# A planned attention and gated feed-forward kernel: new landing estimates for the first transfers and a new table of urgencies

## The chip, the cores and the metric

The kernel runs on one core of one Trainium2 chip. The metric is the device time of one execution in microseconds, as the median of several timed runs. A separate execution, with the hardware profiler on, gives the profile and the trace.

## What is computed

Two parts follow one another. The first is attention without a softmax: queries and keys are projected by two small matrices, the outer product of the two projections is the feature vector of 64 numbers, and the output is a quotient of two sums over keys. The second is a gated feed-forward layer whose gate mixes the rows of the sequence.

```python
def phi(x):
    a = einsum('rd,bhsd->bhsr', S1, x); b = einsum('rd,bhsd->bhsr', S2, x)
    return einsum('bhsi,bhsj->bhsij', a, b).reshape(..., r * r)
kv = einsum('bhsf,bhsd->bhfd', phi(k), v); z = phi(k).sum(2)
x  = (phi(q) @ kv) / (phi(q) @ z + 1e-6)        # heads side by side: (4, 1088, 128)

h = maximum(x @ w_in, 0);  u, v = h[..., :512], h[..., 512:]
v_n = (v - mean(v)) / sqrt(var(v) + 1e-6)
v_s = einsum('ts,bsd->btd', w_spatial, v_n) + b_spatial[:, None]
out = (u * v_s) @ w_out
```

There are 4 batches, 4 heads, 1088 rows, head width 32, model width 128 and hidden width 1024.

## The kernel before

**The work.** Matrices that need full precision are split into a high half (a cast to fp32r) and a low half (the difference). A product is then three matmuls: high by high, high by low, low by high (`mm3`, L439 to L441). Most of the time goes to the spatial product: for each batch b, each block d of 128 gate columns and each group c of output columns (424, 332 and 332 wide), nine k tiles of W are run through, with lines L1011 (high by high), L1013 (low half of v), L1020 and L1022 (low half of W). The tiles of W, their high halves (ScalarE, L563) and low halves (L566, VectorE or GpSimd) are made once, at the beginning. The weights w_in, w_out and the projection matrices arrive as 64-bit numbers, and VectorE makes 32-bit ones of them in some seven instructions (L501 to L514, the first of them on ScalarE for large ones); then come the high half (L518, ScalarE) and the low half (L449, VectorE).

**Batch 0** is prepared with nothing to hide it. Its attention goes through projections (L591), features (L596 on ScalarE, L598 on VectorE), sums over keys (L629), transposes (L717, copied out by L721), sums over features (L731), a division (L735 to L738), a second transpose (L745) and the split of x into halves (L749 on ScalarE, L750 on VectorE). This is done in three groups of 384 rows. Each group then gives three hidden tiles of v (`hidden_v`: `mm3` of 512 columns into the banks `sd`, the ReLU L865 on ScalarE, statistics L867 and L868, the normalization L871 to L890). For batch 0 the normalized tile becomes vh (L955, ScalarE) and vl (L958, VectorE or GpSimd), one k tile after another, and the spatial product of the first column group runs over all four blocks, d = 0 to 3, at once. The gate halves u are products into the one bank `pu`, which ScalarE empties (L1003). Early projections of the queries of batch 1 (L764) stand in the same stretch. L466 is dummy work that keeps PE running where the plan sees it wait.

**Later batches.** Their attention is done beside the spatial product of the batch before. Projected queries go out to memory and come back spread over partitions (the tiles `abd`; L772, L780, L783), GpSimd multiplies them (L784) and makes the low half (L452), and PE uses them in `mm3` into `sd`.

**What sets the order.** Nobody writes the order by hand. Each piece of work is an operation with an engine, a cost, its inputs and outputs and, for PE's main work, a due time. `Order.schedule` first carries the due times backwards to all operations, and takes from each one's due time the value of the table `LEADS` for its name and its group (`o.lead`). It then runs a list scheduler with its own model of the engines: of the operations that can start, each engine takes the one with the earliest due time. Loads (`load`, L446, on the queue of SP) are modelled by their size, one after the other, with eight in flight. The result is one fixed order of instructions for each engine, and a fixed buffer for each tile; the hardware only waits on semaphores. A number in the model or in `LEADS` so changes the order of instructions and nothing else. The assignment of an operation to one of two engines is made by the same planner.

Of the kernel before, what the change touches and what calls it, by code (L numbers as in the profile page):

```python
# [11 lines left out]
U32 = mybir.dt.uint32  # L12
# [65 lines left out]
class T:  # L78
# [8 lines left out]
    @property  # L87
    def ap(self):
        if self._ap is None:
            self._ap = self.k.place(self)  # L90
        return self._ap
# [32 lines left out]
class Order:  # L124
# [13 lines left out]
    def op(self, eng, cost, fn, r=(), w=(), due=None, kb=0, alts=(), sh=False, kind=None, after=0.0, lead=0.0, f4=False, cls=None, lag=0.0):  # L138
# [8 lines left out]
        if kind:  # L147
            o.alts = tuple(a for a in o.alts if a[0] in FORCE.get(kind, [eng]))
            o.eng, _, o.fn = o.alts[0]
            assert o.alts, kind  # L150
        o.stretch, o.sh, o.after, o.lead = self.stretch, sh, after * 1e3, lead + sum(LEADS.get(x, 0) for x in (*self.part, o.name))
        deps = {}
# [49 lines left out]
    def schedule(self):  # L202
# [25 lines left out]
        dma, slow = 0.0, False  # L228
# [5 lines left out]
        while left:  # L234
            best = None
            for e, os in avail.items():
                can = []
                lo = 1e18
                for o in os:
                    s = max(free[e], self.ready_at(o, e))  # L240

                    if e == "POOL":
                        s = max(s, shared_to - 40)
# [5 lines left out]
                    for tag, ts in need.items():  # L249
                        n = len(ts)  # L250
# [3 lines left out]
                        s = max(s, slots[tag][n - 1][0])  # L254
# [3 lines left out]
                if can:  # L258
                    d, s, n, o = min((o.due + STICK * (e == "PE" and o.cls != cls), s, o.n, o) for s, o in can if s <= lo + SLACK[e])
# [4 lines left out]
            s, e, o = best  # L264
            if len(o.alts) > 1:
                s, e = min((self.could_end(o, a, free), a[0]) for a in o.alts)
                s = max(free[e], self.ready_at(o, e), best[0] if e == best[1] else 0)
            _, cost, fn = next(a for a in o.alts if a[0] == e)
            if e == "PE" and s < FILL_TO * 1e3:

                n = int((s - free[e] - FILL_SPARE) // (FILL if s > COLD_TO else FILL_COLD))
# [10 lines left out]
            if e == "PE":  # L282

                s += TURN * (o.f4 != f4)
                f4 = o.f4
                if o.cls != cls or s > free[e] + PAUSE:
                    run = 0
                cls, run = o.cls, run + o.nmm
                settle = SETTLE.get(cls, (0,))
                cost += settle[min(run, len(settle) - 1)] - settle[min(run - o.nmm, len(settle) - 1)]  # L290
                o.end = s + cost + 165
                free[e] = s + cost
            elif e == "SP":
                dma = max(dma, s + cost + 1950) + o.kb / (0.38 if o.kb > 0 else -0.12)

                if dma > 5000 and not slow:
                    slow, dma = True, dma + 1900
                o.end = dma + o.lag
                lanes.append(o.end)
                free[e] = max(s + cost, lanes[-8] if len(lanes) >= 8 else 0)  # L300
            else:
                o.end = s + cost

                if e == "DVE" and o.sh and pool_busy[0] <= s < pool_busy[1] - 20:
                    o.end = max(o.end, pool_busy[1] + cost - 60)
                if e == "POOL":
                    pool_busy = (s, o.end)
                if e == "DVE" and o.sh:
                    shared_to = o.end
                free[e] = o.end - self.OV[e]  # L310
# [36 lines left out]
def c_act(n, psum=False, ptr=False):  # L347
    return (157 if psum else 190) + 0.833 * n + (190 if ptr else 0) if n > 16 else 203


def c_dve(n):
    return 152 + 1.045 * n
# [6 lines left out]
def c_pool(n):  # L359
    return 90 + 2.4 * n  # L360
# [7 lines left out]
def tile_kernel(ctx: ExitStack, tc: tile.TileContext, kT, qT, vA, sks, idn, msk, wT, w_in, w_out, bsp, out):  # L368
# [62 lines left out]
    k = Order(place)  # L431
# [3 lines left out]
    def bank(tag, name):  # L435
        return tl(tag, name, [P, 512])
# [6 lines left out]
    def load(t, ap, src, kb, w=None, **kw):  # L443
        if t.name in FIRST:
            kw["due"] = FIRST.index(t.name) - 1e4
        op("SP", 470, lambda: nc.sync.dma_start(out=ap(), in_=src), w=[w or t], kb=kb, **kw)  # L446

    def sub(o, a, bb):
        return lambda: nc.vector.tensor_tensor(out=o(), in0=a(), in1=bb(), op=ALU.subtract)  # L449

    def sub_pool(o, a, bb):
        return lambda: nc.gpsimd.tensor_tensor(out=o(), in0=a(), in1=bb(), op=ALU.subtract)  # L452
# [3 lines left out]
    z9 = tl(None, "z9", [P, P])  # L456
# [3 lines left out]
    wps = bank("sd", "wps")  # L460
# [9 lines left out]
    eps = tl(None, "eps", [P, 2])  # L470
# [9 lines left out]
    NSK = 2 * H * R  # L480
# [34 lines left out]

    def split(hi, lo, x, n, r, wh, wl, pool=False, due=None, alt=False):

        op("ACT", c_act(n), lambda: nc.scalar.copy(out=hi(), in_=x()), r=r, w=wh)  # L518
        if pool:
            op("POOL", c_pool(n), sub_pool(lo, x, lambda: hi().bitcast(F32)), r=[*r, *wh], w=wl, due=due)  # L520
        else:
            alts = [("POOL", c_pool(n), sub_pool(lo, x, lambda: hi().bitcast(F32)))] if alt else []
            op("DVE", c_dve(n), sub(lo, x, lambda: hi().bitcast(F32)), r=[*r, *wh], w=wl, due=due, sh=True, alts=alts)

    sk = tl(None, "sk", [P, 2 * NSK])
    s_raw = tl("pl", "s_raw", [P, 384])
    load(s_raw, lambda: s_raw[:, :2 * NSK].bitcast(U32), sks.bitcast(U32), 64)
    from_f64(sk, s_raw, NSK)
    ident = tl("abT", "ident_sb", [P, P])
    load(ident, lambda: ident.ap, idn, 64)  # L530

    mask = tl(None, "mask_sb", [P, 6])
    load(mask, lambda: mask.ap, msk, 2)

    kd0 = tl("abT", "kd0", [P, 2, 2, D + 1])

    wTh = tl(None, "wTh", [P, NS, S], F32R)
    wTl = tl(None, "wTl", [P, NS, S], F32R)
    wih = [tl(None, f"wih{j}", [P, DH], F32R) for j in range(2)]
    wil = [tl(None, f"wil{j}", [P, DH], F32R) for j in range(2)]  # L540
    woh = tl(None, "woh", [P, ND, DM], F32R)
    wol = tl(None, "wol", [P, ND, DM], F32R)


    def load_wi(j, raw, x):
        sl = slice(j * 512, j * 512 + 512)
        load(raw, lambda: raw[:, :1024].bitcast(U32), w_in[:, sl].bitcast(U32), 524)
        from_f64(x, raw, 512)
        split(lambda: wih[j].ap, lambda: wil[j].ap, lambda: x[:, :512], 512, [(x, "x")], [wih[j]], [wil[j]])
# [554 lines left out]
    k.part = ("wi1",)  # L1104

    load_wi(1, tl("vt", "wi_raw1", [P, 1024]), tl("vt", "wi_x1", [P, 1024]))
    attention0(sts[0])
    st = sts[0]
# [3 lines left out]
    load_bias()  # L1112
    k.part = ("wi0",)
    load_wi(0, Whole(k, "kt", "wi_raw0", [P, 384]), Whole(k, "v", "wi_x0", [P, 396]))
    k.part = ("wo",)
    load_wo(Whole(k, "kt", "wo_raw", [P, 384]), Whole(k, "v", "wo_x", [P, 396]))
# [62 lines left out]
```

## Time and profile before

| | |
|---|---|
| median of the timed runs | 327.97 us (327.59, 327.98, 327.97) |
| the profiled execution | 328.65 us |
| its span, first to last instruction | 326.8 us |
| TensorE's granted clock in it | 0.999 |
| busy: PE, VectorE, ScalarE, GpSimd | 319.2, 194.3, 152.3, 49.6 us |
| bytes moved | 23.97 MB, 73 GB/s on average |

The clock is full throughout. Busy times of PE are modelled from the starts of pipelined matmuls, so they include the time in which a matmul drains while the next one runs, and small waits hide in them. Columns of transfers and engines by time show a first stretch of some 45 us in which loads, the attention of batch 0 and the preparation of W share all engines, and a long stretch behind it in which PE runs the spatial products.

### The profile page before, as it was taken

Reading aid. Unit: us, or ns where it says so; the run is one execution under the profiler, and the core shown is the slowest. Engines: PE = TensorE matmul, PEld = TensorE weight load, DVE = VectorE, ACT = ScalarE, POOL = GpSimd, SP = SyncE. Lnnn points to the kernel's source line nnn. Section 1 sums busy time; section 2 is a strip of 40 time slices with the busy share of each in tenths; the row PEclk is TensorE's granted clock in tenths of the full one; section 3 lists DMA queues with packets and bytes.
Section 4 is the critical chain, followed back from the end, with each engine's and each line's share of the span. In section 5 each row is a group of like instructions: output and inputs, shape, how many; then the busy total and the mean of one; then the engine's idle time right before and its main releaser. Section 6 shows DMA issues by size and latency. Waiting matters only on the chain.

```text
span 326.8 us, 6680 instructions
## 1 busy us (share of the span) xinstructions
PE 319.2 (98%) x2663; PEld 304.8 (93%) x2663; DVE 194.3 (59%) x437; ACT 152.3 (47%) x358; POOL 49.6 (15%) x60
## 2 busy tenths in 40 slices
PE   8989999999999999999999999999999999999996
PEld 7977899989999899899899999899999999999995
DVE  4889998447689962489984083699544141131023
ACT  2389866634766455366543182764243132121122
POOL 1000100778201005530000730200000000000000
PEclk9999999999999999999999999999999999999999
DMA  6952059674011253400123311000000001000001
GB/s 190 301 170 73 18 157 288 207 214 136 0 38 54 80 179 96 127 2 24 47 70 112 118 41 42 0 2 0 2 1 0 2 27 44 0 0 2 0 2 68
DMA packets 18961, 23.97 MB, mean 73 GB/s; under 512 B 2546, under 2 KB 18674, under 8 KB 18930
## 3 DMA queue, kind: packets, MB, share of 16 engines
q1 hardware_dynamic: 18930, 23.54, 23.5%
q8 instruction: 21, 0.34, 0.5%
q14 instruction: 10, 0.08, 0.1%
HBM read 20.46 MB, written 3.06 MB: 72 GB/s over the span
## 4 chain that ended last, share of the span: by engine, by line
PE 72%; DMA 10%; ACT 5%; DVE 4%; POOL 3%; SPq 2%; issue 2%; POOLq 0%; ACTq 0%
PE sp L1011 16%; PE sp L1020 15%; PE sp L1013 15%; DMA pl<-abd 4%; DMA pl<-in_wT 4%; PE sd L440 3%; PE sd L439 2%; PE sd L441 2%; PE po L439 2%; PE po L441 2%; PE po L440 2%; PE pu L439 2%; DMA v<-in_vA 2%; PE sp L1022 2%; PE pu L441 2%
## 5 line engine op out<-in xcount | busy, mean ns | idle before, releaser
L1011 PE MATMUL sp<-wT,vh 128*128 128x332 f32 (+1 forms) x414 | 133.7, 323 | 0.0
L1013 PE MATMUL sp<-wT,vl 128*128 128x332 f32 (+1 forms) x368 | 118.6, 322 | 0.4 <-DVE vl L958 0.4
L1020 PE MATMUL sp<-wT,vh 128*128 128x332 f32 (+1 forms) x368 | 116.9, 322 | 0.0
L1011 PEld LDWEIGHTS sp<-wT,vh 128*128 128x128 f32 x414 | 77.8, 188 | 1.4 <-issue 0.6
L1013 PEld LDWEIGHTS sp<-wT,vl 128*128 128x128 f32 x368 | 69.2, 188 | 1.2 <-DVE vl L958 0.7
L1020 PEld LDWEIGHTS sp<-wT,vh 128*128 128x128 f32 x368 | 69.0, 188 | 0.2
L1047 DVE TENSOR_TENSOR u<-sp,u 128x332 f32<-128x332 f32 (+1 forms) x40 | 20.6, 517 | 56.4 <-PE sp L1022 47.6
L1003 ACT ACTIVATE u<-pu 128x332 f32<-128x332 f32 (+1 forms) x40 | 18.5, 462 | 30.4 <-PE pu L441 27.7
L867 DVE BATCH_NORM_STATS2 st<-vt 128x6 f32<-128x512 f32 x36 | 24.4, 689 | 11.9 <-ACT vt L865 11.6
L518 ACT CAST g<-u 128x332 fp32r<-128x332 f32 (+1 forms) x38 | 18.1, 484 | 28.3 <-DVE u L1047 18.9
L449 DVE TENSOR_TENSOR g<-u,g 128x332 fp32r<-128x332 f32 (+1 forms) x38 | 20.3, 533 | 15.7 <-PE po L440 9.9
L865 ACT ACTIVATE vt<-sd 128x512 f32<-128x512 f32 x36 | 21.2, 598 | 16.7 <-PE sd L441 16.3
L845 DVE RECIPROCAL c<-c 128x384 f32<-128x384 f32 (+1 forms) x9 | 21.8, 2419 | 7.8 <-ACT c L843 7.6
L784 POOL TENSOR_TENSOR pl<-pl,pl 128x384 f32<-128x384 f32 (+1 forms) x18 | 18.1, 1012 | 53.3 <-DMA pl<-abd 53.3
L927 ACT CAST vh<-vt 128x384 fp32r<-128x384 f32 x36 | 17.7, 510 | 13.3 <-DVE vt L887 10.7
L452 POOL TENSOR_TENSOR r<-pl,r 128x384 fp32r<-128x384 f32 (+1 forms) x18 | 18.6, 1039 | 27.5 <-ACT r L518 27.5
L929 DVE TENSOR_TENSOR vl<-vt,vh 128x384 fp32r<-128x384 f32 (+1 forms) x36 | 17.8, 506 | 2.0 <-ACT vh L927 1.5
L518 ACT CAST r<-pl 128x384 fp32r<-128x384 f32 (+1 forms) x18 | 8.8, 493 | 18.7 <-POOL pl L784 15.3
L598 DVE TENSOR_TENSOR kp<-ka,sd 128x768 f32<-128x768 f32 x15 | 13.7, 948 | 6.0 <-DMA out<-kp 3.6
L563 ACT CAST wT<-pl 128x332 fp32r<-128x332 f32 (+1 forms) x27 | 13.1, 497 | 7.9 <-DMA pl<-in_wT 7.6
L439 PE MATMUL pu<-x,wih 128*128 128x332 f32 (+1 forms) x48 | 16.4, 341 | 0.3 <-ACT u L1003 0.2
L887 DVE TENSOR_SCALAR vt<-vt,mv,sm 128x512 f32<-128x512 f32 x32 | 15.8, 539 | 0.0
(154 smaller groups left out, 500.7 us busy)
## 6 DMA issues: line engine op xcount, KB each, us to landing
pl<-in_wT SPq DMA_DIRECT2D x18, 166.0 KB
v<-in_vA SPq DMA_DIRECT2D x12, 198.0 KB
kt<-in_kT SPq DMA_DIRECT2D x12, 192.0 KB
pl<-abd SPq DMA_DIRECT2D x12, 192.0 KB
pl<-abd SPq DMA_DIRECT2D x24, 96.0 KB
pl<-in_wT SPq DMA_DIRECT2D x9, 212.0 KB
c<-in_qT SPq DMA_DIRECT2D x7, 192.0 KB
out<-u SPq DMA_DIRECT2D x6, 166.0 KB
```

What stands on the lines that cost most here:

```text
L439: nc.tensor.matmul(o, ah, bh, start=start, stop=False)
L441: nc.tensor.matmul(o, al, bh, start=False, stop=stop)
L449: return lambda: nc.vector.tensor_tensor(out=o(), in0=a(), in1=bb(), op=ALU.subtract)
L452: return lambda: nc.gpsimd.tensor_tensor(out=o(), in0=a(), in1=bb(), op=ALU.subtract)
L518: op("ACT", c_act(n), lambda: nc.scalar.copy(out=hi(), in_=x()), r=r, w=wh)
L845: op("DVE", 135 + 6.3 * n, lambda x32=x32, n=n: nc.vector.reciprocal(out=x32[:, :n], in_=x32[:, :n]), w=[x32])
L865: op("ACT", c_act(512, True) + 16, lambda pv=pv, t=t: nc.scalar.activation(vt[:, t], pv.ap, AF.Relu), r=[pv], w=[(vt, t)])
L867: op("DVE", 690, lambda stats=stats, t=t: nc.vector.bn_stats(out=stats.ap, in_=vt[:, t]), r=[(vt, t)], w=[stats])
L1011: nc.tensor.matmul(sp[:, :cw], vh[:, kt], wTh[:, kt, cs], start=(kt == 0), stop=False)
L1013: nc.tensor.matmul(sp[:, :cw], vl[:, kt], wTh[:, kt, cs], start=False, stop=False)
L1020: nc.tensor.matmul(sp[:, :cw], vh[:, kt], wTl[:, kt, cs], start=False, stop=False)
L1047: op("DVE", c_dve(cw), lambda: nc.vector.tensor_tensor(out=u.ap, in0=sp[:, :cw], in1=u.ap, op=ALU.mult), r=[sp], w=[u], lead=LEAD[1])
```

## The change

Three numbers of the planner's model of the transfers are other ones, and the table of urgencies is a new one. It had 1577 entries and has 1581; of the 1748 names in the two, 1739 have another value. The table is one line; its first entries stand for it here.

```diff
-LEADS = {'W0': -5650, 'W0.0': 9780, 'W0.1': -16100, 'W0.2': -13770, 'W0.3': 10920,
...
+LEADS = {'W0': -19300, 'W0.0': 11900, 'W0.2': -16500, 'W0.3': 14820, 'W0.4': 2800,
...
                 if dma > 5000 and not slow:
-                    slow, dma = True, dma + 1900
+                    slow, dma = True, dma + 1400
...
-    load(s_raw, lambda: s_raw[:, :2 * NSK].bitcast(U32), sks.bitcast(U32), 64)
+    load(s_raw, lambda: s_raw[:, :2 * NSK].bitcast(U32), sks.bitcast(U32), 64, lag=-800, due=-1e6)
...
-        load(raw, lambda: raw[:, :1024].bitcast(U32), w_in[:, sl].bitcast(U32), 524)
+        load(raw, lambda: raw[:, :1024].bitcast(U32), w_in[:, sl].bitcast(U32), 1000 if j else 1160)
```

The load of the projection matrices is planned to land 0.8 us sooner and to be issued first; the two halves of w_in are planned as if they had 1000 and 1160 KB (they have 512 KB each, as before); a delay that the plan adds once, early, is 1.4 us and was 1.9.

The same instructions run on the same engines, but for three pairs of normalizations of batch 0 (L887 on VectorE, L890 on ScalarE) that change places, and for the dummies L466, 16 and not 17. The order of the first loads is nearly what it was. The order on the engines differs in many places. Three of them follow.

ScalarE, in the attention of batch 0, behind the copies of the first transposes (`ka`, the last feature copy; `wih`, the high half of the second half of w_in; `kt` and `v`, where the first half of w_in lands and is converted; `c`, copies of transposes; `wT`, high halves of W; `x`, the high half of x). Before:

```order
L596 COPY ka_69<-sd_91 128x96
L501 ACTIVATE v<-kt 128x512
L518 CAST wih_280<-vt_165 128x512
L563 CAST wT<-pl_213 128x424
L518 CAST bh<-b_64 83x16
L563 CAST wT<-pl_229 128x424
L563 CAST wT<-pl_238 128x424
L721 COPY c_112<-po_266 128x384
L721 COPY c_146<-po_148 128x384
L563 CAST wT<-pl_251 128x424
L749 CAST x<-sp_308 128x384
```

Now:

```order
L596 COPY ka_69<-sd_91 128x96
L518 CAST wih_276<-vt_162 128x512
L501 ACTIVATE v<-kt 128x512
L721 COPY c_116<-po_265 128x384
L721 COPY c_146<-po_148 128x384
L563 CAST wT<-pl_215 128x424
L563 CAST wT<-pl_230 128x424
L518 CAST bh<-b_64 83x16
L749 CAST x<-sp_310 128x384
```

The cast of `wih` has moved ahead of L501, the two copies L721 ahead of the casts of W, and one cast of W fewer stands before L749.

PE at the end of batch 0's attention, behind the third turn of x (L745; `pu` is the gate bank, `po` with `u` the early queries, `sd` the hidden tiles of v). Before:

```order
L745 MATMUL sp_308<-abT_121,c_163 128x128 x3
L439 MATMUL pu_174<-x,wih_67 128x424
L440 MATMUL pu_174<-x,wih_67 128x424
L441 MATMUL pu_174<-x,wil_71 128x424
L764 MATMUL po_247<-u_277,sk 64x160 x2
L466 MATMUL po_266<-z_83 128x64
L439 MATMUL sd_126<-wih_280,x 128x512
L440 MATMUL sd_126<-wil_290,x 128x512
L441 MATMUL sd_126<-wih_280,x 128x512
```

Now:

```order
L745 MATMUL sp_310<-abT_131,c_160 128x128 x3
L439 MATMUL pu_176<-x,wih_67 128x424
L440 MATMUL pu_176<-x,wih_67 128x424
L441 MATMUL pu_176<-x,wil_71 128x424
L466 MATMUL po_265<-z_83 128x64 x2
L439 MATMUL pu_176<-x,wih_67 128x424
L440 MATMUL pu_176<-x,wih_67 128x424
L441 MATMUL pu_176<-x,wil_71 128x424
L439 MATMUL sd_124<-wih_276,x 128x512
L440 MATMUL sd_124<-wil_288,x 128x512
L441 MATMUL sd_124<-wih_276,x 128x512
```

The early queries L764 have left this place; all of them now stand earlier, the first four between the last transposes L717 and the first turn of x. The gate product of block 2 has moved up to here, and that of block 3, which stood among the first column group's spatial product, follows before that product begins.

VectorE at the first k tiles of the spatial product, from the low half of the second k tile on (`vl`; the third is GpSimd's; `st`, `mv`, `sm` are statistics; `v` with L504 is a conversion of w_out; `bl` is the low half of the bias). Before:

```order
L958 TENSOR_TENSOR vl<-vt_344,vh 128x512
L867 BN_STATS st_381<-vt_165 128x6
L887 TENSOR_SCALAR vt_104<-vt_104,mv_415,sm_456 128x512
L868 BN_AGGR mv_486<-st_381 128x2
L958 TENSOR_TENSOR vl<-vt_104,vh 128x512
```

Now:

```order
L958 TENSOR_TENSOR vl<-vt_346,vh 128x512
L878 SCALAR_TENSOR_TENSOR sm_491<-mv_414,sm_453 128x3
L868 BN_AGGR mv_493<-st_362 128x2
L867 BN_STATS st_374<-vt_162 128x6
L868 BN_AGGR mv_493<-st_356 128x2
L868 BN_AGGR mv_493<-st_374 128x2
L887 TENSOR_SCALAR vt_104<-vt_104,mv_414,sm_453 128x512
L504 TENSOR_SCALAR v<-v 128x512
L873 RECIPROCAL sm_518<-sm_510 128x3
L449 TENSOR_TENSOR bl<-b_64,bh 83x16
L878 SCALAR_TENSOR_TENSOR sm_522<-mv_493,sm_518 128x3
L958 TENSOR_TENSOR vl<-vt_104,vh 128x512
```

The low half of the second tile has moved ahead of small instructions, which now stand between it and the low half of the fourth tile, with L504 and the bias.

2 lines of the change are left out of this document (1 added, 1 removed).

## The prediction

> **What bounds the kernel now.** I read the head of the page first, then the waits of TensorE (PE), the windows, and the timelines of each engine where PE waits.
>
> ```profile
> span 326.8 us, 6680 instructions
> ...
> PE 319.2 (98%) x2663; PEld 304.8 (93%) x2663; DVE 194.3 (59%) x437; ACT 152.3 (47%) x358; POOL 49.6 (15%) x60
> ```
>
> PE is busy 98% of the span, so nothing but PE's own waits and dummy work can be saved: the matmuls are the same before and after. Its waits, longest in total first:
>
> ```profile
> PE sd L462 <- DVE z L458: 1.3, 1, 1.3
> PE sp L745 <- DVE c L738: 0.8, 1, 0.8
> PE sd L440 <- POOL r L452: 0.5, 1, 0.5
> PE sd L439 <- ACT vt L865: 0.5, 1, 0.5
> PE sp L1013 <- DVE vl L958: 0.4, 1, 0.4
> ...
> PE pu L439 <- ACT u L1003: 0.2, 1, 0.2
> ```
>
> The reader is to see how little there is: 1.3 us is the start, 0.8 stands in the attention of batch 0 (L745), 0.4 at the second k tile of the first spatial product (L1013), and about 1.2 later. But busy PE also hides dummy matmuls and a refill behind each wait. What decides how early the real work can begin is another engine:
>
> ```profile
> 20.00:30.00 10.00, 10.00 (x65) 7.91 (x64) 9.73 (x30) 8.93 (x20) 0.00 (x0) 1.00 0.36 106
> 30.00:40.00 10.00, 9.62 (x48) 8.55 (x48) 9.75 (x30) 8.52 (x20) 1.29 (x1) 1.00 0.06 13
> ...
> 50.00:60.00 10.00, 10.00 (x124) 9.48 (x123) 6.44 (x14) 6.06 (x16) 0.94 (x2) 1.00 0.88 284
> ```
>
> The columns are PE, PEld, VectorE (DVE), ScalarE (ACT), GpSimd (POOL). From 20 to 40 us VectorE is busy 9.7 us of every 10, ScalarE 8.5 to 8.9. There PE follows these two, and from 50 to 60 the transfers are near full (0.88). So a change of order pays if ScalarE and VectorE come to the same instructions earlier.
>
> **Step 1: ScalarE no longer stands in front of a transfer.** (Timeline rows: start, duration, engine, line, operation, tiles; in brackets the idle time before and what ended it. SPq is the queue that issues transfers.)
>
> ```profile
> 15.59 0.69 ACT L501 ACTIVATE v<-kt 128x512 f32<-128x512 f32 x1 [1.20 <-DMA u<-in_qT]
> 16.18 0.60 ACT L518 CAST wih<-vt 128x512 fp32r<-128x512 f32 x1
> 17.03 0.55 ACT L563 CAST wT<-pl 128x424 fp32r<-128x424 f32 x1 [0.25 <-DMA pl<-in_wT]
> ...
> 18.55 0.85 ACT L721 COPY c<-po 128x384 f32<-128x384 f32 x2
> ...
> 19.74 0.49 ACT L749 CAST x<-sp 128x384 fp32r<-128x384 f32 x1
> ```
> ```profile
> 14.17 0.69 DVE L514 TENSOR_TENSOR vt<-vt 128x512 f32<-128x512 f32 x1
> ...
> 15.85 0.17 DVE L735 TENSOR_SCALAR rec<-sp 128x12 f32<-128x12 f32 x1
> 16.82 0.69 DVE L449 TENSOR_TENSOR wil<-vt,wih 128x512 fp32r<-128x512 f32 x1 [0.80 <-ACT wih L518]
> ...
> 20.27 0.56 DVE L750 TENSOR_TENSOR x<-sp,x 128x384 fp32r<-128x384 f32 x1 [0.44 <-ACT x L749]
> ```
> ```profile
> 18.44 0.55 PE L745 MATMUL sp<-abT,c 128*128 128x128 f32 x3 [0.80 <-DVE c L738]
> ...
> 19.46 1.45 PE L731 MATMUL sp<-abT,c 128*128 128x66 f32 x12
> 20.73 0.48 PE L439 MATMUL sd<-wih,x 128*128 128x512 f32 x1
> ...
> 22.30 0.87 PE L764 MATMUL po<-u,sk 128*64 128x192 f32 x8
> ```
> ```profile
> 16.46 0.35 SPq L446 DMA_DIRECT2D u<-in_qT  x1
> ```
>
> Before, ScalarE is free at 14.39 (15.59 less the wait of 1.20) and waits with L501 for the load of the second half of w_in. The cast of wih1 (L518) is queued behind it, though VectorE had its input ready at 14.86 (14.17 + 0.69). In the new order the cast is first: 14.9 to 15.5, and L501 still starts at 15.6, when its load is there, so the move costs nothing. VectorE's low half of the weights (L449) then follows L735 at 16.02 instead of 16.82: 0.80 us earlier, and with it the divided result that L745 turns.
>
> Behind L501 the two copies L721 now come first (16.2 to 17.05; before at 18.55, behind three casts of W and that of bh). They free the banks for the last transposes and for the early query projections L764, 0.87 us of PE work that moves from 22.30 to a place where PE ran dummies and waited. Their loads are in time: the third load of this kind takes the queue lane of the second and is issued at 16.46, so the second had landed by then. L764 so ends at 17.9, and L745 starts at about 18.0, not 18.44. The cast L749 can follow at once (18.6, since only two casts of W and bh stand before it, done at 18.1) and not at 19.74; L750 comes 0.53 behind it as before: 19.15 against 20.27, **1.1 us earlier for VectorE**. PE's first hidden product (20.73) comes after L745 and the 1.27 us of sums (L731, 19.46 to 20.73): at 19.85, 0.9 earlier. I take 1.0 for both. The path behind is VectorE's, which does the same work up to the third group of rows, so the 1.0 stays. Bounds: 0.44 (the gain at L745 alone) and 1.1.
>
> **Step 2: work moved into the wait ahead of the first spatial product.**
>
> ```profile
> 32.95 0.35 PE L1011 MATMUL sp<-wT,vh 128*128 128x424 f32 x1
> ...
> 35.23 0.46 PE L1013 MATMUL sp<-wT,vl 128*128 128x424 f32 x1 [0.38 <-DVE vl L958]
> ...
> 42.62 0.35 PE L439 MATMUL pu<-x,wih 128*128 128x424 f32 x1
> ...
> 43.19 0.35 PE L1011 MATMUL sp<-wT,vh 128*128 128x424 f32 x1
> ```
> ```profile
> 30.20 0.64 ACT L955 CAST vh<-vt 128x512 fp32r<-128x512 f32 x1
> 30.81 0.30 ACT L871 ACTIVATE sm<-mv,eps 128x3 f32<-128x3 f32 x1
> 31.01 0.50 ACT L1003 ACTIVATE kp<-pu 128x424 f32<-128x424 f32 x1
> ```
> ```profile
> 32.68 0.14 DVE L878 SCALAR_TENSOR_TENSOR sm<-sm,sm 128x3 f32<-128x3 f32 x1
> ...
> 33.35 1.10 DVE L878 SCALAR_TENSOR_TENSOR sm<-mv,sm 128x3 f32<-128x3 f32 x1
> ...
> 34.53 0.65 DVE L958 TENSOR_TENSOR vl<-vt,vh 128x512 fp32r<-128x512 f32 x1
> ...
> 36.54 0.69 DVE L958 TENSOR_TENSOR vl<-vt,vh 128x512 fp32r<-128x512 f32 x1 [0.22 <-ACT vh L955]
> ...
> 38.68 0.59 DVE L566 TENSOR_TENSOR wT<-pl,wT 128x424 fp32r<-128x424 f32 x1
> ...
> 39.26 0.42 DVE L504 TENSOR_SCALAR v<-v 128x512 f32<-128x512 f32 x1
> ```
> ```profile
> 33.13 1.29 POOL L958 TENSOR_TENSOR vl<-vt,vh 128x512 fp32r<-128x512 f32 x1 [30.78 <-ACT vh L955]
> ```
>
> The gate product of block 3 (three matmuls, 43.19 - 42.62 = 0.57 us, 0.19 each) is now done before the spatial product. It gives ScalarE one more L1003 (0.50) ahead of the first cast of vh (L955, 30.20), so the start moves to 32.95 - 1.0 + 0.5 = 32.45.
>
> The second k tile: before, L1013 at 35.23 stands 2.28 behind the start. Nine matmuls at 0.19 are 1.71, so 0.57 are lost (0.38 of wait, the rest refill). Its input was ready at 35.18 (34.53 + 0.65). Now VectorE is 1.0 earlier, has the L878 that took 1.10 behind this instruction, no longer before it, and one more L566 (0.59) before it: 35.18 - 1.0 - 1.10 + 0.59 = 33.67. PE needs it at 32.45 + 1.71 = 34.16. The wait goes, with 0.49 to spare. PE is then 1.07 earlier and has 0.57 of work more behind it: **1.64 us**.
>
> The fourth k tile is tight. Its low half ended at 37.23 (36.54 + 0.69). VectorE leads by 1.51 at the second tile (35.18 - 33.67), but the 1.10 and L504 (0.42) now stand between the two: 37.23 - 1.51 + 1.10 + 0.42 = 37.24. PE, after twelve pairs of matmuls, asks for it at 32.45 + 4.56 + 0.19 = 37.2. I take no loss; the bound is 1.0 (0.42 + 0.59, all of it waited for).
>
> **A rule of the Trainium skill, weighed here.** The L878 of 1.10 us is a three-column instruction; its like at 32.68 took 0.14. It ended at 34.45, when GpSimd's 1.29 us instruction from 33.13 had ended (34.42). The Trainium skill, page "SBUF — State Buffer", section "SBUF: two separate sides", says that VectorE instructions with two inputs in SBUF and GpSimd instructions exclude one another for their whole length, whoever starts first. By that rule, the trace agrees, and it speaks against this order: the next such VectorE instruction is now the low half of the second k tile itself. The second rival below is this case; the sum would be 327.1 by it, and not 326.3.
>
> **Step 3: the later waits.** Some 1.2 us by the list above:
>
> ```profile
> 72.26 1.16 POOL r L452
> ```
>
> (A row of the chain of work that ended last: start, duration, what.) This step of a chain, in which the query features come by DMA and GpSimd takes them, ends the 0.5 us wait of L440 at 73. PE comes there 1.64 earlier. GpSimd's queue begins now with the first tile of the third column group, where it stood before the third tile, so its chain should come as much earlier; the loads near full speed are what could hold it. The other later waits meet an order that is new in every batch. I see some that go and cannot see those that come: 0 for all. Bounds: 1.2 gained, 1.5 lost (as much again and a little). The last instructions of all engines are in the same order, so the end costs the same.
>
> **The sum.** 1.64 off the profiled span of 326.8 is 325.2; the profiled execution took 328.65, so 327.0 for a profiled run. The timed median, 327.97, is 0.68 below that execution: **326.3 us**. Dummies are 16 instead of 17, worth 0.1 at most, and left out.
>
> **The rivals.**
> - **All of it, and the later waits too**: 1.64 + up to 1.2, some 325.1. For it: the 0.5 us wait of L439 for ScalarE hangs on hidden products that stand later among PE's work in the new order. Chance 0.13.
> - **GpSimd first**: its instruction starts before VectorE's low half of the second tile, which then is ready at 33.67 + 1.29 = 34.96, not by 34.16: 0.80 lost, 327.1. The margin is what GpSimd's start (one cast of 0.6 behind the one VectorE needs) leaves, so this may well be. Chance 0.15.
> - **The gain is waited away** at 73 us or at a ScalarE queue later: if the chain quoted in step 3 moves 0.5 only, PE waits 1.1 more and the whole is 327.5. This is also the case that the new numbers do not do what they say, as better estimates of landings are of no use where other waits decide. It lies within 0.2% of before (0.66 us, about what a measurement can tell from no change). Chance 0.20.
> - **Slower: ScalarE's order at the start of the spatial product.** L871, which waits for VectorE's statistics of the second group, stood behind the first cast of vh (30.81 behind 30.20). Now it stands before it, with L890 and two L1003 queued behind; each microsecond by which the statistics come late moves the start of PE's main work by one. The statistics were there by 30.81, so with VectorE's 1.0 by 29.8, and as VectorE now makes them ahead of L750 and L887 I reckon with 29.0. If L871 starts later than 30.64, the 1.64 are gone; from 31.3 the kernel is slower by over 0.2%, and at 31.5 it takes 328.8. That needs VectorE to lose its lead and 0.5 more. Chance 0.09.
>
> **Chances.** The forecast itself, 325.6 to 327.2, has 0.43. Faster by over 0.2%: 0.43 + 0.13 + 0.15 = 0.71, of which 0.01 falls inside 0.2%: 0.70. Same 0.20 + 0.01, slower 0.09. The range is 324.4 (1.64 with all later waits gone and the dummies, and some beyond) to 328.3 (all gains waited away and a little more).
>
> **What would show it.** Right: L518 on wih ahead of L501 near 14.9; L745 near 18.0 and L750 near 19.15; the first L1011 near 32.5; no wait at the second k tile's L1013; the last matmul about 1.6 earlier. Wrong: L764 waiting for its loads in front of L745; a VectorE L958 that takes over 1 us; waits of PE from 36 to 45 us, or longer ones than 0.5 at 70 to 75 us or behind ScalarE later. The forecast fails above all if the later waits add up to more than before.

## The result, and the profile after

| | before | after |
|---|---|---|
| median of the timed runs | 327.78 us (4 runs) | **330.9 us** (330.15 to 332.11, 4 runs) |
| ratio to before | | **1.0104**, 95% interval 1.0068 to 1.0141 |
| profiled execution, its span | 328.65, 326.8 us | 330.7, 328.9 us |

The changed kernel is 1% slower; 326.3 us was forecast. The same kernel again, twelve times: 330.24 us, ratio 1.0071 (1.0047 to 1.0096). One kernel's executions spread: before took 326.71 to 330.06 us in the 31 of one group. A profile therefore shows places, and medians of many runs show sums. Executions over 1.5% above the fastest one of the same kernel are left out of the ratios, but not of the medians, so where the two differ below, the ratio is the one to go by.

PE's waits in the changed kernel (engine, line, what ended the wait: us in all, times, longest):

```profile
PE pu L439 <- ACT u L1003: 1.8, 2, 1.5
PE sd L462 <- DVE z L458: 1.3, 1, 1.3
PE po L441 <- issue: 0.6, 1, 0.6
PE po L440 <- DVE g L449: 0.5, 1, 0.5
PE sd L591 <- DVE kp L598: 0.4, 1, 0.4
PE pu L439 <- ACT kp L1003: 0.3, 1, 0.3
PE sp L1013 <- DVE vl L958: 0.3, 1, 0.3
```

The 0.8 at L745, the 0.5 for GpSimd and the 0.5 at L865 are gone, as hoped. The longest is a new one, 1.5 us of L439 for ScalarE's L1003, and there are four smaller new ones. The timeline of the start, PE first, then VectorE and ScalarE:

```profile
7.75 2.67 PE L466 MATMUL po<-z 128*128 128x64 f32 x22
10.35 0.92 PE L629 MATMUL pu<-v,kp 128*64 128x66 f32 x24
...
18.63 0.55 PE L745 MATMUL sp<-abT,c 128*128 128x128 f32 x3
```
```profile
16.51 0.68 DVE L449 TENSOR_TENSOR wil<-vt,wih 128x512 fp32r<-128x512 f32 x1
...
19.72 0.56 DVE L750 TENSOR_TENSOR x<-sp,x 128x384 fp32r<-128x384 f32 x1 [0.21 <-ACT x L749]
```
```profile
8.01 0.67 ACT L501 ACTIVATE vt<-vt 128x512 f32<-128x512 f32 x1
...
15.54 0.62 ACT L518 CAST wih<-vt 128x512 fp32r<-128x512 f32 x1 [0.57 <-DVE vt L514]
```

L518 is ahead of L501 as forecast, but at 15.54, not 14.9, since the chain in front of it is late: PE runs 22 dummy matmuls (11 pairs) until L629 starts at 10.35. Before there were 12 (6 pairs) in this place, and L629 started at 9.64 after a wait for its load. The added dummies come with the plan's new numbers (shown below), by which w_in lands later; in this execution L501 found its half of w_in there at 8.01. Now the spatial product and the place at 60 us:

```profile
32.99 0.36 PE L1011 MATMUL sp<-wT,vh 128*128 128x424 f32 x1
...
38.43 0.46 PE L1013 MATMUL sp<-wT,vl 128*128 128x424 f32 x1 [0.27 <-DVE vl L958]
...
60.20 0.42 PE L439 MATMUL pu<-x,wih 128*128 128x332 f32 x1 [1.46 <-ACT u L1003]
```
```profile
33.54 0.67 DVE L958 TENSOR_TENSOR vl<-vt,vh 128x512 fp32r<-128x512 f32 x1
34.13 1.27 DVE L878 SCALAR_TENSOR_TENSOR sm<-mv,sm 128x3 f32<-128x3 f32 x1
...
37.68 0.69 DVE L958 TENSOR_TENSOR vl<-vt,vh 128x512 fp32r<-128x512 f32 x1
```
```profile
33.73 1.64 POOL L958 TENSOR_TENSOR vl<-vt,vh 128x512 fp32r<-128x512 f32 x1 [31.38 <-ACT vh L955]
```
```profile
35.43 1.52 ACT L890 ACTIVATE vt<-vt,sm,sm 128x512 f32<-128x512 f32 x2 [0.92 <-DVE sm L878]
...
37.05 1.65 ACT L955 CAST vh<-vt 128x512 fp32r<-128x512 f32 x3
...
56.98 0.47 ACT L563 CAST wT<-pl 128x332 fp32r<-128x332 f32 x1 [1.77 <-DMA pl<-in_wT]
58.87 0.93 ACT L563 CAST wT<-pl 128x332 fp32r<-128x332 f32 x2 [1.42 <-DMA pl<-in_wT]
59.71 0.44 ACT L1003 ACTIVATE u<-pu 128x332 f32<-128x332 f32 x1
```

The second k tile's wait is gone (L958 at 33.54), and one at the fourth has come: L878 holds L890, that L955, that the L958 of 37.68. At 60 us the one gate bank is full; the L1003 that empties it stands in ScalarE's queue behind two casts of W whose loads are late (before, this L1003 stood there too, but PE's next gate product came 2.3 us of work later).

**Where the time went.** I take PE's lag: the time at which PE has done W us of its work, each matmul at its usual spacing, less W. It grows where PE waits, idles or runs dummies L466. Its size hangs on the spacings taken, the difference of two kernels hardly. After less before, from the two profiles:

| W (us of work) | 20 | 30 | 45 | 50 | 65 | 70 | 160 | end |
|---|---|---|---|---|---|---|---|---|
| lag before | 8.29 | 9.83 | 10.14 | 10.28 | 12.33 | 12.33 | 15.56 | 17.54 |
| lag after | 7.51 | 9.50 | 10.19 | 12.01 | 12.64 | 13.47 | 17.36 | 19.62 |
| difference | -0.78 | -0.33 | +0.05 | +1.73 | +0.31 | +1.14 | +1.80 | +2.08 |

The forecast was -0.9, -1.64 and -1.64 in the first three columns and -1.64 from there on. So two things failed: 1.7 us by 45 us of work, and the rest, 2.0 here, behind it. How they divide differs from execution to execution: a second profile of the changed kernel (the last run below) is 0.3 ahead of before at W = 45 and 0.1 behind at the end, so there it is 1.3 and 0.5.

### The profile page after: what moved, and what is told of

Read it like the earlier page. It is cut to its first block, busy times and chain, and to the rows that moved or that the text cites. A ratio compares the mean times of both kernels' runs of the same rounds, so it can differ in the third digit from the quotient of the medians.

```text
span 328.9 us, 6669 instructions
## 1 busy us (share of the span) xinstructions
PE 320.2 (97%) x2661; PEld 304.9 (93%) x2661; DVE 197.9 (60%) x437; ACT 153.0 (47%) x358; POOL 49.5 (15%) x60
## 4 chain that ended last, share of the span: by engine, by line
PE 83%; DVE 8%; ACT 5%; DMA 2%; issue 1%; DVEq 0%
PE sp L1011 18%; PE sp L1013 16%; PE sp L1020 16%; PE sd L439 3%; PE sd L441 2%; PE sd L440 2%; PE pu L439 2%; PE po L440 2%; PE po L441 2%; PE sp L1022 2%; PE po L439 2%; PE pu L441 2%; PE pu L440 2%; DMA pl<-in_wT 2%; PE sd L591 1%; PE sd L641 1%
## 5 line engine op out<-in xcount | busy, mean ns | idle before, releaser
L1011 PE MATMUL sp<-wT,vh 128*128 128x332 f32 (+1 forms) x414 | 134.8, 326 | 0.1
L1013 PE MATMUL sp<-wT,vl 128*128 128x332 f32 (+1 forms) x368 | 119.1, 324 | 0.3 <-DVE vl L958 0.3
L1011 PEld LDWEIGHTS sp<-wT,vh 128*128 128x128 f32 x414 | 77.9, 188 | 3.3 <-issue 1.3
L1013 PEld LDWEIGHTS sp<-wT,vl 128*128 128x128 f32 x368 | 69.2, 188 | 1.0 <-DVE vl L958 0.5
L1003 ACT ACTIVATE u<-pu 128x332 f32<-128x332 f32 (+1 forms) x40 | 18.5, 462 | 36.6 <-PE pu L441 33.5
L518 ACT CAST g<-u 128x332 fp32r<-128x332 f32 (+1 forms) x38 | 18.2, 483 | 25.1 <-DVE u L1047 24.4
L449 DVE TENSOR_TENSOR g<-u,g 128x332 fp32r<-128x332 f32 (+1 forms) x38 | 22.5, 591 | 7.2 <-ACT g L518 5.6
L865 ACT ACTIVATE vt<-sd 128x512 f32<-128x512 f32 x36 | 21.5, 599 | 11.2 <-PE sd L441 10.7
L452 POOL TENSOR_TENSOR r<-pl,r 128x384 fp32r<-128x384 f32 (+1 forms) x18 | 17.8, 1003 | 32.3 <-ACT r L518 31.7
L439 PE MATMUL pu<-x,wih 128*128 128x332 f32 (+1 forms) x48 | 16.3, 340 | 2.1 <-ACT u L1003 1.8
L518 ACT CAST r<-pl 128x384 fp32r<-128x384 f32 (+1 forms) x18 | 8.8, 495 | 17.9 <-POOL pl L784 17.8
L1047 DVE TENSOR_TENSOR kp<-sp,kp 128x424 f32<-128x424 f32 x6 | 3.6, 598 | 22.1 <-PE sp L1022 22.1
L887 DVE TENSOR_SCALAR vt<-vt,mv,sm 128x512 f32<-128x512 f32 x32 | 15.9, 539 | 0.0
```

The lines of the kernel that those rows point to most:

```text
L439: nc.tensor.matmul(o, ah, bh, start=start, stop=False)
L865: op("ACT", c_act(512, True) + 16, lambda pv=pv, t=t: nc.scalar.activation(vt[:, t], pv.ap, AF.Relu), r=[pv], w=[(vt, t)])
L1011: nc.tensor.matmul(sp[:, :cw], vh[:, kt], wTh[:, kt, cs], start=(kt == 0), stop=False)
L1013: nc.tensor.matmul(sp[:, :cw], vl[:, kt], wTh[:, kt, cs], start=False, stop=False)
L1047: op("DVE", c_dve(cw), lambda: nc.vector.tensor_tensor(out=u.ap, in0=sp[:, :cw], in1=u.ap, op=ALU.mult), r=[sp], w=[u], lead=LEAD[1])
```

## The experiments

The edits work on the finished order of the plan: an operation is put ahead of another on its engine, dummies are left out, or a tile gets a buffer of its own; everything else stays. Each ratio is to the kernel before, run on the same chip.

### Three edits to the changed kernel

ScalarE at 57 us (first run), PE's dummies (second), VectorE at 32 us (the third edit, in the fourth run):

```diff
 L563 CAST wT<-pl_281 128x332
+L1003 ACTIVATE u_199<-pu_176 128x332
 L563 CAST wT<-pl_245 128x332
 L563 CAST wT<-pl_215 128x332
-L1003 ACTIVATE u_199<-pu_176 128x332
```
```diff
-L466 MATMUL po_148<-z_83 128x64 x11
+L466 MATMUL po_148<-z_83 128x64 x6
 L629 MATMUL pu<-v,kp_141 64x66 x12
```
```diff
+L878 SCALAR_TENSOR_TENSOR sm<-mv,sm 128x3
 L867 BN_STATS st<-vt 128x6 x2
 L958 TENSOR_TENSOR vl<-vt,vh 128x512
-L878 SCALAR_TENSOR_TENSOR sm<-mv,sm 128x3
```

L1003 moved:

> The changed kernel with one instruction moved: on ScalarE the L1003 that empties the gate bank after the first gate product of the second column group stands ahead of two L563 casts of W that wait for their loads, not behind them. Theory A (PE's new waits make up the loss, and each comes back whole when it goes): the wait of 1.46 us at 60.2 us goes with its refill of 0.18, so 330.9 - 1.6 = 329.3 us. Rival B (what PE gains here it waits away at 73 us): in the changed kernel GpSimd's low half for the first query product was ready some 0.46 us before PE asked for it, so only 0.46 stays: 330.4 us, with a wait of about 1 us of L440 for GpSimd at 73 us.

Five dummies (pairs) fewer:

> The changed kernel with 5 of the 11 dummies (10 of 22 matmuls L466) ahead of the first sum over keys (L629) taken out; before the change there were 6. Theory A: these dummies, and nothing else, hold L629 back from about 9.6 us to 10.35, and with it the cast L518 and the first hidden product, so the first L1011 of the spatial product starts at 32.4 instead of 33.0; but the wait at 60.2 us hangs on loads of W that land when they do, so it grows by 0.6 and the time stays 330.9 us. Rival B (the loads go with PE, as their buffers come free earlier): 330.3 us. Rival C (L629 waits for its load, not for the dummies): it starts at 10.3 still, 330.9 us.

Both:

> Both edits of the two runs before: L1003 ahead of two casts, and 5 dummies fewer. Theory A (gains add up once the wait at 60 us is gone): 330.9 - 1.6 - 0.6 = 328.7 us. Rival B (waited away at 73 us): 330.4 us, with a wait there of 1.5 us or more.

All three:

> The two edits and a third: on VectorE the small L878 that waits for the port beside GpSimd's L958 (1.27 us at 34.1) moved up by three places, ahead of two L867, where GpSimd does not run yet. Theory A: it then takes 0.15 us, ScalarE's L890 behind it starts about 1 us earlier, the fourth k tile's low half is there in time, and the PE wait at 38.4 us (0.65 with its refill) goes: 328.1 us. Rival B: another instruction of VectorE (an L867 or an L958) takes the long wait for GpSimd in its place, nothing moves: as the run with two edits.

| edit | median us | ratio, 95% interval |
|---|---|---|
| L1003 moved | 331.33 | 1.0095 (1.0061 to 1.0130) |
| dummies | 329.15 | 1.0030 (1.0010 to 1.0050) |
| both | 328.7 | 1.0008 (0.9984 to 1.0032) |
| all three | 327.8 | 1.0007 (0.9983 to 1.0031) |

**L1003 alone brings nothing**: neither 329.3 nor the 0.46 of theory B. PE did not wait at 60 us; its lag was 1.8 us smaller than the changed kernel's at W = 100 (12.68 against 14.46) and the same at 120 (14.95, 14.98). It was lost at a place that neither theory had:

```profile
126.43 0.46 PE L439 MATMUL pu<-x,wih 128*128 128x424 f32 x1 [0.91 <-ACT u L1003]
```
```profile
125.93 0.45 ACT L1003 ACTIVATE u<-pu 128x332 f32<-128x332 f32 x1 [3.93 <-DMA out<-u]
```

(Timelines of the run with L1003 moved.) This L1003 writes a buffer out of which an earlier output tile is stored. Its store was issued at 120.00 us here, 0.82 earlier than in the changed kernel, and L1003 could go at the same time in both, 125.9.

**The dummies bring most**, 1.1 to 1.75 us by the medians, more than the 0.6 expected. L629 starts at 9.26, the spatial product at 31.88, 1.1 earlier than 32.99:

```profile
7.78 1.55 PE L466 MATMUL po<-z 128*128 128x64 f32 x12
9.26 0.92 PE L629 MATMUL pu<-v,kp 128*64 128x66 f32 x24
```

Theory B, that loads move with PE, is nearer than A: the wait at 60 us did not grow (0.65, between the 1.46 and 0.56 of the two profiles of the changed kernel).

**Both** come to the 328.7 us of theory A by luck: the dummies brought more than its 0.6 and L1003 less than its 1.6. **All three together undo the loss**, as theory A had said to 0.3 us; by the ratio the first two already do (1.0008 and 1.0007), and between the second and the fourth run the steps (0.45 and 0.9 by the medians, 0.7 and nothing by the ratios) are within the intervals. In the profiles the third edit makes PE's lag 0.9 smaller at W = 45, and at 65 nothing of it is left. With all three, PE is 1.9 ahead of before at W = 45, more than the 1.64 of the forecast, and 0.2 ahead at the end. The L878 behaved as theory A says (VectorE, then GpSimd, of that run):

```profile
31.23 0.16 DVE L878 SCALAR_TENSOR_TENSOR sm<-mv,sm 128x3 f32<-128x3 f32 x1
31.30 1.28 DVE L867 BATCH_NORM_STATS2 st<-vt 128x6 f32<-128x512 f32 x2
32.50 0.68 DVE L958 TENSOR_TENSOR vl<-vt,vh 128x512 fp32r<-128x512 f32 x1
```
```profile
32.50 1.83 POOL L958 TENSOR_TENSOR vl<-vt,vh 128x512 fp32r<-128x512 f32 x1 [30.15 <-ACT vh L955]
```

0.16 and not 1.27, and there is no wait at the fourth k tile.

### One part of the change alone; the dummies added to the kernel before

> Only the three numbers of the planner's model of transfers, with the table of urgencies of before. Theory A (the new numbers bring the dummies: the plan sees the first values land later and fills the time): 11 dummies ahead of L629, which starts at 10.3 us, 328.7 us or more. Rival B (the estimates help by themselves): at or below 328.0 us.

> Only the new table of urgencies, with the three numbers of before. 6 dummies ahead of L629. Theory A (the loss is shared: without the dummies the table alone still brings the waits behind 45 us): about 329.2 us, as the changed kernel with 5 dummies fewer. Rival B (the table is bound to the numbers it was found with; elsewhere its order is a random one): 330 us or more, with waits at new places. Rival C (the loss is the numbers' alone): 328.0 us or less.

> The kernel before the change with 5 dummies (10 matmuls L466) more ahead of the first sum over keys L629: 11 as in the changed kernel, where it had 6. Nothing else moves. Theory A (these dummies, planned against a landing that comes sooner, are the largest single loss, and what starts late stays late): L629 starts at 10.3 instead of 9.6 us, and the time grows by about as much as it fell when they were taken out of the changed kernel (330.9 to 329.15): 328.7 (0.7 more, what the start shows) to 329.7 (1.75 more). Rival B (later waits hide it: PE waits 0.8 us for VectorE at L745 anyway): 328.0 us, no change.

The three numbers with the old table: **333.83 us** (1.0197, 1.0167 to 1.0226). L629 starts at 10.33, behind 11 dummies, and among the waits are 1.7 for L1003 and 1.0 for a late cast of vh. The new table with the old numbers: **340.94 us** (1.0394, 1.0364 to 1.0424), with 5.0 us of waits for L1003 in five places. So rival B of the second holds: a table of urgencies belongs to the numbers it was found with, and neither part can be judged alone (each mixture is slower than either whole). That the dummies come with the numbers is shown by the first; with which of the three, and how much of its 6 us they are, is not.

In the kernel before, with its dummies raised to 11, L629 starts at 10.05 and the median is 328.73 against 327.93 (1.0017, 0.9996 to 1.0037): at most 1.2 us. In the profile of before PE waits 0.8 for VectorE at L745 anyway, and with 11 pairs this wait is gone, so it covered part. The changed order has no such wait left to cover them.

### The prediction's steps by hand in the kernel before

Step 1 on ScalarE, step 2 on VectorE (with it, on ScalarE, the second k tile's L955 ahead of the third's), and the later query product:

```diff
+L518 CAST wih<-vt 128x512
 L501 ACTIVATE v<-kt 128x512
-L518 CAST wih<-vt 128x512
+L721 COPY c<-po 128x384 x2
 L563 CAST wT<-pl 128x424
...
-L721 COPY c<-po 128x384 x2
```
```diff
+L878 SCALAR_TENSOR_TENSOR sm<-mv,sm 128x3
+L958 TENSOR_TENSOR vl<-vt,vh 128x512
 L867 BN_STATS st<-vt 128x6
-L878 SCALAR_TENSOR_TENSOR sm<-mv,sm 128x3
 L868 BN_AGGR mv<-st 128x2 x2
-L958 TENSOR_TENSOR vl<-vt,vh 128x512
```
```diff
+MOVES = (("sp021:9", "nd100:1"), ("po01:1", "nd100:1"), ("sp031:1", "nd100:1"), ("sp031:2", "nd100:1"))
```

(In the last, each first operation goes ahead of the second: `sp` is a k tile of the spatial product, `po` an output product, `nd100` the query product.)

> The kernel before with step 1 of the prediction alone: on ScalarE the cast L518 of the second half of w_in ahead of L501, and the two copies L721 behind L501, ahead of the casts of W. Theory A (the step works as forecast and its gain reaches the end): L518 at 14.9 us, L449 at 16.0, L745 near 17.7, spatial product about 1 us earlier, 327.0 us. Theory B (the step works, and the gain is waited away at places that go by loads, at 61 to 74 us or at 127 us): start of the spatial product about 1 us earlier, 327.7 to 328.2 us. Rival C (the step fails: L501 or the casts of W, now later, hold PE elsewhere before 33 us): start not earlier, 328.0 us.

> The kernel before with the two steps of the prediction put in by hand and nothing else: step 1 as in the run that had it alone (328.19 us), and for step 2 the second k tile's low half L958 on VectorE ahead of an L867 and of two L868, the L878 that took 1.10 us ahead of it, before GpSimd's L958 starts (on ScalarE the second k tile's high half is cast ahead of the third's). Theory A (steps 1 and 2 hold, step 3 fails: what PE gains is waited away at places that go by transfers): start of the spatial product 0.9 us earlier and no wait at the second k tile, 1.4 us ahead at 50 us, but longer waits at 61 to 74 us; 327.7 to 328.2 us. Rival B (the prediction's sum): 326.3 us. Rival C (the L958 or the L878 still meets GpSimd and takes over 1 us): 328.0 us with the wait at the second k tile.

> The run before, with eleven matmuls (1.6 us: the last k tile of block 2, an output product, two k tiles of block 3) ahead of the first query product of batch 1, so that PE comes later to the place where it waits for GpSimd at 73 us. Theory A (that wait is where the gain of the two steps went): no wait there, 326.3 to 327.0 us. Rival B (the gain is taken back at the next such place, at 127 to 139 us): 327.7 to 328.2 us.

> The kernel before with steps 1 and 2 by hand (327.27 us) and with 3 dummies ahead of L629 where there were 6. Theory A: L629 starts as its values land, 326.8 us. Rival B: as the run with 6, 327.3 us.

| kernel before with | median us | ratio, 95% interval |
|---|---|---|
| step 1 | 328.19 | 1.0002 (0.9983 to 1.0021) |
| steps 1 and 2 | 327.27 | 0.9974 (0.9951 to 0.9997) |
| and query product later | 327.64 | 0.9988 (0.9966 to 1.0010) |
| steps 1 and 2, and 3 dummies fewer | **326.86** | **0.9968** (0.9943 to 0.9994) |

Step 1 works and brings nothing that can be measured: L518 stands at 14.90, the spatial product starts at 32.01, 0.94 earlier; the lag is 0.93 smaller than before at W = 25, but 0.55 at 45 (a longer spacing of matmuls, last section) and 0.30 at 65. The start and the time are those of theory B; of its places less is seen: 0.4 of the gain is gone by W = 45, ahead of the first place that it names, and 0.25 goes between there and 65. Step 2 by hand works too (run with both steps):

```profile
31.53 0.16 DVE L878 SCALAR_TENSOR_TENSOR sm<-mv,sm 128x3 f32<-128x3 f32 x1
31.70 0.69 DVE L958 TENSOR_TENSOR vl<-vt,vh 128x512 fp32r<-128x512 f32 x1
```

The product starts at 31.62, no k tile is waited for, and the lag at W = 45 is 8.56 against 10.14: 1.58, the forecast's 1.64 all but 0.06. Of this the median keeps 0.7, more than theory A has and less than rival B. Where the rest goes is not shown: the profile is of the shortest of the twelve executions (326.11 us), and in it the lead is still there at the end. Moving the query product out of its wait for GpSimd did not help: PE then waits 0.76 at 78.44 us for a VectorE step (L449) instead. The run with three dummies fewer is the fastest version, faster than both kernels; against the run with six the 0.4 is within the intervals.

### Where the gain at 60 us is lost

The edits are the buffer, in the first three runs; the k tiles ahead of the query product, in the third alone; and in the fourth, without the buffer, 8 pairs of dummies fewer and not 5. The fifth run is the changed kernel once more.

```diff
+OWN = {"ob02": 3}
+MOVES = (("sp011:7", "nd100:1"), ("sp011:8", "nd100:1"), ("sp011:9", "nd100:1"))
-DROP = {"kv0:1": 5}
+DROP = {"kv0:1": 8}
```

> As the run with L1003 ahead of two casts (331.33 us), and the output tile of the third column group of batch 0 has a buffer of its own, so that the gate tile that follows it no longer waits for its store (DMA out<-u, which ended a wait of 3.9 us of L1003 at 125.9 us; PE waited 0.91 for that L1003 at 126.4). Theory A (the gain of the move was alive at 100 us, 1.8 us in the profile, and was lost to this store): no PE wait at 126 us, 329.5 us. Rival B (PE waits as long for something else there, GpSimd's L452 at 128 us first): 331 us, as without the buffer.

> The run with three edits (327.8 us) and the buffer of its own for the output tile of the third column group of batch 0; nothing moved at 71 us. Theory A (the store that lands at 124 us, by which L1003 waits 2.9 us and GpSimd's L452 comes late, costs PE 0.67 at 126.8 us): that wait is gone, 327.1 us. Rival B (the 0.67 is waited elsewhere, GpSimd's own transfers come as late): 327.8 us.

> As the run with three edits (327.8 us; L1003 ahead of two casts, 5 dummies fewer, L878 ahead of two L867), with the buffer of its own for that output tile, and with the last three k tiles of block 1 (eight matmuls, 1.2 us) ahead of the first query product of batch 1, which waited 1.02 us for GpSimd at 71 us. Theory A: the waits at 71 us (1.28 with the refill) and at 126 us (0.67) go and nothing comes in their place: 326.0 to 326.6 us, below the kernel before. Rival B (a later wait takes them back, as at 138 or 193 us): 327.3 to 328 us.

> The run with three edits (327.8 us) with 8 dummies fewer ahead of L629 and not 5: 3 are left. Theory A (dummies hold L629 back to 9.1 us also in executions in which its load is there sooner): L629 starts as its values land, between 8.4 and 9.2 us, and the time falls by up to 0.5: 327.3 us. Rival B (VectorE's seven instructions on w_in set the pace from here, ScalarE's copy L596 waits 0.2 only): 327.7 us.

> The changed kernel once more, beside the three others of this group, as their common base. Theory (its 11 dummies end after any landing of the first values, so L629 starts within 10.0 to 10.4 us whether w_in lands at 8.0 or at 9.1 us; the losses behind 45 us hang on transfers): 330.9 us, L629 at 10.0 to 10.4, PE waits again for L1003 at 58 to 60 us. Rival (it was a slow session of one chip): 329 us or less.

With the buffer, L1003 moved: 330.54 us (1.0083, 1.0049 to 1.0118), not 329.5; its profile, with a granted clock of 0.852, shows nothing of the place. With three edits and the buffer: 329.98 us, ratio 1.0005 (0.9966 to 1.0043), no better than without the buffer (1.0007). In its profile the wait at 126.8 us is gone, and at the next gate product one comes (PE, ScalarE, GpSimd),

```profile
138.10 0.42 PE L439 MATMUL pu<-x,wih 128*128 128x332 f32 x1 [1.80 <-ACT u L1003]
```
```profile
136.70 0.51 ACT L518 CAST r<-pl 128x384 fp32r<-128x384 f32 x1 [3.66 <-POOL pl L784]
...
137.60 0.45 ACT L1003 ACTIVATE u<-pu 128x332 f32<-128x332 f32 x1
```
```profile
134.79 1.87 POOL L784 TENSOR_TENSOR pl<-pl,pl 128x320 f32<-128x320 f32 x2 [1.08 <-DMA pl<-abd]
```

again an L1003 in ScalarE's queue behind a step that waits for GpSimd and, through it, for transfers. Behind this wait the granted clock fell as well (last section). With the query product later as well: 329.05 us (1.0021, 0.9995 to 1.0047), no better than without: its profile has new waits at 59 to 82 us, for L449, L518 and L1003. So each time the wait came back elsewhere, as theory B says, though the last of the three times (329.05) is above its range. With three dummies left instead of six: 327.73 us (0.9988, 0.9964 to 1.0011), the same within its interval, though L629 starts as its values land:

```profile
8.57 0.92 PE L629 MATMUL pu<-v,kp 128*64 128x66 f32 x24 [0.47 <-DMA v<-in_vA]
```

The changed kernel again: 330.24 us, and L629 at 9.97 with w_in landed at 8.42, at 10.35 with w_in there by 8.01 (first profile). Its wait at 60 us was 0.56, not 1.46:

```profile
58.92 0.42 PE L439 MATMUL pu<-x,wih 128*128 128x332 f32 x1 [0.56 <-ACT u L1003]
```

## Why the prediction was wrong

- **Step 1, the start: right in kind, late by the dummies.** The cast is ahead of L501, L745 came at 18.63 (18.0 forecast), L750 at 19.72 (19.15), the first hidden product at 20.27 (19.85). The 14.9 for L518 took VectorE's input at the time of before. (The load that L501 waited for before is that of the first half of w_in, `kt`, and not of the second, as step 1 has it; the sum does not change by this.) The failed line is "Dummies are 16 instead of 17, worth 0.1 at most, and left out": I counted them and did not look where they stood. The order shows 11 pairs in a row ahead of L629, where it showed 6. That is the largest single loss that an edit brought back, 1.1 to 1.75 us by the medians.
- **The gate product moved forward** cost 0.5 of ScalarE in the sum. It also met the one gate bank: PE runs four dummy matmuls and waits 0.3 for L1003 ahead of the third gate product at 29.64. For the start at 32.99, not 32.45, the dummies are enough: with five pairs fewer it is 31.88, though 0.38 of that is a load that landed sooner than before (L629 at 9.26, not 9.64). What the gate product costs is not shown by itself.
- **Step 2, second k tile: right.** L958 ended at 34.21 and no wait is left. **The fourth k tile: "I take no loss; the bound is 1.0"** was wrong by 0.65 (0.27 of wait, the rest refill). The path in the profile ran from L878 (1.27) over ScalarE's L890 and L955 to L958. VectorE's own queue, which I had followed, would have been there only 0.14 sooner (37.54): the same L878 held it. With that L878 moved the wait is gone.
- **The port rule.** The Trainium skill, page "SBUF — State Buffer", section "SBUF: two separate sides", was weighed against this order; the trace agrees with it. GpSimd's 1.64 us instruction began at 33.73, after VectorE's L958 of 33.54, and the L878 behind took 1.27, until 35.40, when GpSimd's had ended (35.37). In the run with three edits both start at 32.50 and GpSimd's takes 1.83. So my second rival, GpSimd first, did not happen; whom the wait hits decides, and here it was a short instruction with a long chain behind it.
- **Step 3, "0 for all", failed, and it is what is left when the start and the fourth k tile are mended.** Its bound was 1.5 lost; behind W = 45 the first profile of the changed kernel shows 2.0 lost, the second 0.5. In the run with all three edits PE is 1.9 ahead at W = 45 and loses 1.7 of it behind. One of the places is the chain at 73 us (GpSimd and PE of that run):

```profile
70.21 1.96 POOL L452 TENSOR_TENSOR r<-pl,r 128x384 fp32r<-128x384 f32 x2
```
```profile
71.26 0.44 PE L440 MATMUL sd<-r,kvh 128*128 128x384 f32 x1 [1.02 <-POOL r L452]
```

L452 comes 2.0 earlier than before (72.22), so the chain did move as much as PE, as step 3 said, but PE still waits 1.02 for it where it waited 0.52. In the changed kernel itself PE came too late to wait there. A new wait at 59 to 60 us (1.46 and 0.56 in its two profiles) has the shape of my third rival, a ScalarE queue later, which I had priced as the loss of the gain and not as more.

- **The rivals.** L871 started at 29.64, well before the 30.64 from which the slower rival counts: that mechanism was not it. The kernel was slower for another reason, which no rival named.
- **Open.** How the loss behind 45 us divides among its places is not settled. Taking one wait away moved it to another twice, and these places differ from execution to execution. The sum also stood on one profile of before, and that execution (328.65) is 0.7 us over the median.

## What to carry to other kernels

A dummy, or any filler placed by a plan, is a wait of fixed length: find where each stands before and after, and what is behind it, instead of counting them. Where a measured landing goes into a plan, ask which of several executions it comes from, as a plan set to a late one starts late in all. And a gain made early may be waited away at a later place whose time is set by transfers; carry it to the end place by place, or claim a part of it.

## What the runs showed of the hardware that was not expected

**The same load lands over 1 us apart.** The second half of w_in, which is loaded first, is issued at 2.59 or 2.60 us, and ScalarE's L501 waits for it. In two runs of the changed kernel's order, with the same loads in the same order, L501 was released by it at 9.03 us (three edits, buffer, query product later) and at 7.99 (three dummies left):

```profile
9.03 0.66 ACT L501 ACTIVATE vt<-vt 128x512 f32<-128x512 f32 x1 [0.71 <-DMA vt<-in_w_in]
```
```profile
7.99 0.66 ACT L501 ACTIVATE vt<-vt 128x512 f32<-128x512 f32 x1 [0.42 <-DMA vt<-in_w_in]
```

In other runs of this order it was at 8.42 and 8.70, and in the profile of before, whose loads stand in a slightly other order, at 9.06.

**The same matmuls follow one another at two spacings**, with no wait and the clock at 1.00. Windows of before and of after (us, PE busy and its matmuls, clock, share and GB/s of transfers):

```profile
39.00:43.00 4.00, 4.00 (x24) 1.00 0.43 115
```
```profile
39.00:43.00 4.00, 4.00 (x22) 1.00 0.33 70
```

The 128x424 matmuls of L1011 and L1013 started every 0.187 us in the first and every 0.196 in the second. Before, the spacing became short at the wait for the second k tile; after, it stayed long until 43.6 us, which made up 0.45 us of the lost 1.7. In the run with step 1 alone it stayed long behind the same wait, so a wait alone does not decide it; the cause is open.

**The granted clock fell behind some short waits of PE.** In the run with three edits and the buffer PE idled 1.80 us until 138.10, and then (columns as above):

```profile
130.00:140.00 10.00, 8.20 (x47) 0.98 0.37 107
140.00:150.00 10.00, 10.00 (x49) 0.85 0.01 2
```

By these shares 1.7 us of clock were lost (an estimate: 2% and 15% of 10 us), about as much as the wait itself. In the run of the new table with the old numbers the clock was 0.66 from 209 to 214 us, behind a wait of 1.05 that ended at 207.77. Behind one of 1.96 that ended at 179.43 in the same run, and behind the 1.46 at 60.20 of the changed kernel, it stayed at 1.00. What decides is open.
